# An attention and maxout kernel: a branch on the head flags, with two key blocks per query block for the odd heads in one arm

## The chip, the cores and the metric

The kernel runs on one core of a Trainium2 chip. The metric is the device time of that core in microseconds, from the first to the last instruction of one execution. Five engines work side by side: TensorE (PE in the profile; its weight loads are listed apart as PEld), VectorE (DVE), ScalarE (ACT), GpSimd (POOL) and SyncE (SP), which here only issues transfers. Each engine takes its instructions in the order in which they are written. Transfers are issued by SP, ACT and POOL and carried by 16 DMA engines.

## The reference

Causal attention for 4 batches, 8 heads, 768 positions and a head size of 64 is followed by a maxout layer. A head that is flagged as a retrieval head sees all earlier positions. Any other head, a streaming head, sees the first 4 positions (the sink) and the last 64 (the window).

```python
is_retrieval = np.array([1, 0, 1, 0, 0, 0, 1, 0])
n_sink, window = (4, 64)
causal = rel >= 0                       # rel = query position - key position
stream_keep = causal & (is_sink | ((rel >= 0) & (rel < window)))
scores = np.where(mask, scale * q @ k.T, -1e9)     # mask: causal, or stream_keep, by head
a = exp(scores - max) / (sum + 1e-9)
x = (a @ v) as 3072 tokens x 512
out = maximum(maximum(x @ w1, x @ w2), x @ w3) @ w_out      # 512 -> 768 -> 512
```

The flags are an input of the kernel, so what is computed must hold for any flags. In these inputs heads 0, 2 and 6 are retrieval heads, and all odd heads and head 4 are streaming heads.

## The kernel before

**Tiles.** A batch is cut into two halves of 384 queries, and a half into three query blocks of 128. Keys lie in blocks of 128 too. Work on the scores is numbered by t = 4 * batch + 2 * half + qd, where qd names one of two groups of four heads; a group holds two pairs of heads, i = 0 and 1. Scores are made with keys in the rows and queries in the columns. A score unit (`scores`, L553 for the matmuls) computes up to 512 such columns for each head of the group; which key and query blocks stand in which unit is told by `UNITS`. One half's causal triangle has 6 blocks in two units, the second half's has 15 in four. In batch 0 two heads of a pair use 64 rows each of the array side by side; in the other batches four heads use 32 rows each, and a block takes two passes (head size 64 = 2 x 32), which add up in PSUM. ScalarE then takes the exponential of a unit and writes fp16 (`pt`, L564).

**Masks.** `mk` holds a mask of 512 columns for each head, made from the head's flag (L389). VectorE or GpSimd multiplies the blocks near the diagonal and at the start with it (`masks`, L586). For the far blocks of streaming heads the values are scaled instead: `vf` is the values times `far`, which is zero there but for the sink's rows (`prep_v`, L504 and L506). So one instruction stream serves all flags, and streaming heads compute all of their causal blocks.

**Values and layer.** `av` (L602) multiplies a weight tile, a 128x128 block of `pt`, with 65 columns of values (the last is a one, for the sum), over all key blocks up to the query block, and divides (L610, L612). The result is turned by a DMA transpose (L621) or by TensorE (`turn_x`), and feeds the layer: `ffn` (L438 for the three projections, L455 and L458 for the maximum, L474 for the output product, L480 for the copy to the output tile).

**Order.** Nothing is scheduled at build time: `PROGRAM` is an order written out item by item, and each item issues its instructions on its engines at that place. `s t u i` is a score unit, `k` a mask, `v` the preparation of values, `av` the product with the values, `x` the turning, `f` the next piece of the layer, which fills TensorE between score units, `load`, `load_v` and `hl` are loads, `w` weights, `turn` and `turnp` the turning of keys and queries, `em` and `m` the masks for each head, `idle n` runs n matmuls on zeros. Loads of batch 0 and of all values go through SP's queue; weights, and the keys and queries of the other batches, through GpSimd's. Tiles come from pools that are used in turn.

Of the kernel before, what the change touches and what calls it, by code (L numbers as in the profile page):

```python
# [37 lines left out]

APART = [(0, 0, 1, (384,), 128, 0), (1, 1, 1, (384,), 128, 0)] + MASKED[1][1:]


EARLY = 0

FIRST = "hl 0 0 1, ir"

PROGRAM = (
    "idle 2, idle 8, cast 0 0 aa, hl 0 1 1 ss, hl 0 2 2 ss, read, hl 1 0 2 ss, cast 0 1 pp",
    "flags, cast 0 2 ap, em 1, turnp 0 1 a, far, em 0, turnp 0 0 aa, cast 0 3 da, em 2, em 3",
    "load_v 0 0 4 4, s 0 0 1, s 0 0 0, v 1 1 pp, cast 1 1 pa, turnp 0 3 dd, turnp 0 2 da",
    "w 0 2 0, load_v 0 0 0 4, v 0 0 dp, s 1 0 0, w 0 2 1, s 0 1 0 b, hl 1 2 2 ss, s 1 0 1",  # L50
    "cast 1 2 dp, v 1 0 dd, s 0 1 1, s 1 1 0 b, av 0 0, v 0 1 pp, turnp 1 1 a, s 1 1 1",
    "turnp 1 2 aa, x 0 0 a, s 2 0 1, cast 1 0 dp, load_v 0 1, cast 1 3 ad, av 1 1, s 2 1 1",
    "av 1 0, x 1 1 d, av 0 1, turnp 1 0 ad, s 2 2 1, x 1 0 d, s 3 0 0, m 0, w 1, x 0 1 d",
    "s 2 0 0, m 3, m 1, f 1 d, f 1 d, s 2 1 0, s 2 2 0, m 2, f 1 a, f 1 d, k 2 1 2 p, k 2 0 1 d",
    "w 2, f 1 d, s 2 3 1, load 1 0, w 3, k 3 0 0 d, s 3 1 0, f 1 a, s 2 3 0, load 1 1",
    "k 2 0 3 p, k 2 0 2 p, turnp 1 3 dd, k 3 0 1 p, k 2 1 1 d, k 2 1 3 d, f 1 d, f 1 d",
    "v 2 0 ad, f 1 a, f 1 a, v 3 1 pp, f 1 d, s 3 0 1, v 2 1 dp, s 3 1 1, f 1 a, v 3 0 ap",
    "av 2 0 D, f 1 d, f 1 d, s 3 2 0, turn 1 0 0 0, turn 1 0 0 1, f 1 a, turn 1 0 1 0, s 3 2 1",
    "s 3 3 0, k 3 0 2 p, k 3 1 2 p, turn 1 0 1 1, f 1 a, av 2 1 D, s 3 3 1, k 3 1 1 d",
    "k 3 0 3 p, k 3 1 3 p, f 1 a, k 3 1 0 d, load_v 1 0, gate, f 1 a, s 4 0, k 4 1 0 p",  # L60
    "v 4 0 pp, av 3 0, av 3 1, f 1 a, f 1 a, x 3 0 d, s 4 1, turn 1 1 0 1, x 3 1 a, f 1 d",
    "v 5 1 pp, turn 1 1 1 0, turn 1 1 1 1, turn 1 1 0 0, k 4 0 1 d, k 4 0 0 d, k 4 1 1 p, f 1 a",
    "f 1 a, f 1 d, load_v 1 1, f 1 a, f 1 a, f 1 a, v 4 1 pd, f 1 a, f 1 d, s 5 0, f 1 a, f 1 d",
    "av 4 0 D, k 5 0 0 d, f 1 d, s 5 1, k 5 0 1 p, load_v 2 0, f 1 a, f 1 a, load 2 0, f 1 a",
    "s 6 0, f 1 d, av 4 1 D, f 1 a, v 5 0 ap, f 1 a, s 6 1, f 1 a, av 5 0 D, f 1 d, f 1 d",
    "k 5 1 1 p, k 5 1 0 p, v 7 0 dp, s 6 2, k 6 1 2 p, f 1 a, av 5 1 D, turn 2 0 1 0, f 1 a",
    "v 6 0 ad, s 6 3, turn 2 0 0 1, x 5 1 d, f 1 a, turn 2 0 1 1, load 2 1, load 3 1",
    "load_v 2 1, v 6 1 ap, f 1 d, f 1 d, k 6 0 2 p, v 9 0 ap, k 6 1 3 p, f 1 a, f 1 a",
    "turn 2 0 0 0, s 7 0, f 1 a, f 1 d, f 1 d, turn 2 1 0 0, k 6 0 1 d, f 1 a, s 7 1, f 1 d",
    "f 1 a, f 1 a, k 6 1 1 p, k 7 1 1 d, f 1 d, s 7 2, f 1 a, f 1 a, k 6 0 3 p, k 7 1 2 d",  # L70
    "turn 2 1 1 0, load 3 0, av 6 0 D, s 7 3, f 1 d, v 7 1 pp, av 6 1 D, k 7 1 3 p, f 1 d",
    "turn 3 1 1 0, k 7 0 3 p, turn 2 1 0 1, s 8 0, k 7 0 1 p, turn 2 1 1 1, k 7 0 2 p, f 1 a",
    "f 1 d, load_v 3 0, k 8 0 0 p, av 7 1 D, s 8 1, f 1 a, f 1 a, s 9 0, v 8 0 ap, k 8 0 1 d",
    "f 1 a, f 1 d, av 7 0 D, v 13 1 pp, s 9 1, f 1 a, av 8 0 D, f 1 d, s 10 0, f 1 a, x 7 1 d",
    "f 1 a, v 10 0 dd, f 1 d, s 10 1, f 1 a, f 1 d, v 9 1 ad, f 1 a, f 1 d, f 1 a, s 10 2",
    "f 1 d, f 1 d, f 1 d, k 8 1 0 p, f 1 d, k 9 0 0 p, k 9 1 1 d, f 1 d, f 1 d, v 11 0 ad",
    "f 1 d, k 9 1 0 p, v 12 0 ad, k 9 0 1 p, k 8 1 1 d, av 9 0 D, v 8 1 ap, s 10 3, f 1 d",
    "f 1 a, av 8 1 D, turn 3 0 1 0, s 11 0, k 10 1 1 p, f 1 d, f 1 d, k 10 0 3 p, f 1 a",
    "av 9 1 D, v 13 0 ap, f 1 a, k 10 1 3 d, turn 3 0 1 1, x 9 1 a, k 10 0 1 p, s 11 1, f 1 a",
    "k 10 0 2 p, v 11 1 ap, av 10 0 D, f 1 d, s 11 2, k 11 0 2 p, turn 3 0 0 0, f 1 a",  # L80
    "turn 3 0 0 1, f 1 d, k 11 0 1 d, f 1 a, k 10 1 2 d, f 1 d, v 10 1 ap, f 1 a, turn 3 1 0 1",
    "f 1 a, f 1 a, s 12 0, av 10 1 D, f 1 a, f 1 d, k 12 1 0 p, s 12 1, f 1 d, f 1 a, f 1 a",
    "k 12 0 1 p, turn 3 1 0 0, s 11 3, v 12 1 ad, f 1 a, load_v 3 1, f 1 a, f 1 a, k 11 0 3 d",
    "k 11 1 3 p, f 1 d, f 1 d, k 11 1 1 p, turn 3 1 1 1, f 1 a, f 1 d, av 11 0 D, f 1 d",
    "k 11 1 2 d, f 1 a, k 12 0 0 p, k 12 1 1 d, f 1 a, s 13 0, av 12 0 D, f 1 d, av 11 1 D",
    "k 13 0 0 d, f 1 d, f 1 d, s 13 1, f 1 d, v 15 1 pp, f 1 d, k 13 0 1 p, x 11 1 d, f 1 d",
    "v 15 0 ad, av 12 1 D, k 13 1 1 d, av 13 0 D, s 15 0, f 1 a, f 1 d, f 1 d, f 1 a, f 1 d",
    "f 1 d, f 1 a, k 13 1 0 d, s 15 1, v 14 0 ap, f 1 d, f 1 a, f 1 d, f 1 d, s 14 0, f 1 a",
    "f 1 d, f 1 d, f 1 d, av 13 1 D, s 14 1, f 1 d, x 13 1 d, f 1 d, f 1 d, f 1 a, f 1 a",
    "s 14 2, f 1 a, k 14 1 2 p, v 14 1 ad, k 14 1 1 p, f 1 d, f 1 d, f 1 d, f 1 a, f 1 a",  # L90
    "k 15 0 1 p, s 14 3, f 1 d, k 14 0 3 p, f 1 a, f 1 d, s 15 2, f 1 a, f 1 d, f 1 d, f 1 d",
    "s 15 3, f 1 a, k 15 1 1 d, f 1 a, k 15 1 3 d, f 1 a, k 15 1 2 d, k 14 0 1 p, f 1 a",
    "k 14 0 2 p, k 14 1 3 p, k 15 0 3 d, av 14 0 D, f 1 a, f 1 a, f 1 a, av 14 1 D, f 1 a",
    "f 1 d, k 15 0 2 p, av 15 1 D, f 1 a, av 15 0 D, f 1 d, x 15 1 d, f 1 a, f 1 d, f 1 a",
    "f 1 d, f 1 d, f 1 a, f 1 a, f 1 a, f 1 d, f 1 a, f 1 a, f 1 d, f 1 d, f 1 a, f 1 d, f 1 a",
    "f 1 a, f 1 a, f 1 a, f 1 a, f 1 d, f 1 a, f 1 d, f 1 a, f 1 d, f 1 a, f 1 d, f 1 a, f 1 a",
)

# [11 lines left out]
def kernel(  # L110
# [14 lines left out]
    nc = tc.nc  # L125
# [14 lines left out]
    assert (S, D, DMdl) == (768, 64, 512) and window <= P and n_sink <= P  # L140
# [5 lines left out]

    consts = ctx.enter_context(tc.tile_pool(name="consts", bufs=1))
    stage = ctx.enter_context(tc.tile_pool(name="stage", bufs=3))
    pairs2 = ctx.enter_context(tc.tile_pool(name="pairs2", bufs=2))
    once = ctx.enter_context(tc.tile_pool(name="once", bufs=1))  # L150
    half16 = ctx.enter_context(tc.tile_pool(name="half16", bufs=3))
    qkt = ctx.enter_context(tc.tile_pool(name="qkt", bufs=3))
    ptp = ctx.enter_context(tc.tile_pool(name="ptp", bufs=5))
    xp = ctx.enter_context(tc.tile_pool(name="xp", bufs=4))
    xtp = ctx.enter_context(tc.tile_pool(name="xtp", bufs=3))
    htp = ctx.enter_context(tc.tile_pool(name="htp", bufs=2))
    accp = ctx.enter_context(tc.tile_pool(name="accp", bufs=7))
    fwork = ctx.enter_context(tc.tile_pool(name="fwork", bufs=3))
    sps = ctx.enter_context(tc.tile_pool(name="sps", bufs=2, space=bass.MemoryType.PSUM))
    bkp = ctx.enter_context(tc.tile_pool(name="bkp", bufs=4, space=bass.MemoryType.PSUM))  # L160

    ctx.enter_context(tc.manual_schedule())


# [5 lines left out]
    def bank(shape, dtype, name):  # L170
        return bkp.tile(shape, dtype, tag="bank", name=name)

    staged = {}
    cast = {}
    KQs = {}

    def load_pairs(half, hp, n, engines):
        for nm, src, eng in zip(("ks", "qs"), (k, q), engines):  # L180
            st = (
                pairs2.tile([P, 4, HB, D], FP32, tag=nm, name=nm) if n == 2
                else once.tile([P, 2 * n, HB, D], FP32, name=f"{nm}{hp}")
            )
            m = 2 * n if eng is nc.gpsimd else 2
            for h in range(0, 2 * n, m):
                eng.dma_start(  # L187
                    out=st[:, h : h + m],
                    in_=src[
                        0, 2 * hp + h : 2 * hp + h + m, half * HALF : (half + 1) * HALF  # L190
                    ].rearrange("h (p j) d -> p h j d", p=P),
                )
            for i in range(n):
                staged.setdefault((half, hp + i), []).append(st[:, 2 * i : 2 * i + 2])

    def load_cast(half, hp, n):
        for nm, src in (("kc", k), ("qc", q)):
            st = half16.tile([P, 4, HB, D], FP16, tag=nm, name=nm)
            nc.gpsimd.dma_start(
                out=st[:, 0 : 2 * n],  # L200
                in_=src[
# [215 lines left out]
    def ffn(b, half):  # L417
# [31 lines left out]
        if early:  # L449
            yield  # L450
# [265 lines left out]
```

## Time and profile before

| | |
|---|---|
| Median of 3 runs | 200.72 us (199.87 to 202.32) |
| The profiled execution | 199.87 us; span 199.9 us, so nothing lies around the span |
| Mean granted clock of TensorE | 0.990 of full speed |
| Bytes | 25.17 MB read from HBM, 6.29 MB written |
| Value products (L602) | 352 with `va` and 320 with `vf` |
| Score matmuls (L553) | 560 |
| Masks of `pt` (L586) | 54 on GpSimd, 57.3 us; 32 on VectorE, 14.3 us |
| Exponentials (L564) | 98, 83.3 us |

In the profile's lists a group of instructions has its busy time, in which instructions that overlap on a pipelined engine count once, and the mean duration of one, which for matmuls holds the whole way through the array. The chain that ended last is shown in pieces: start, length, engine, tile and line. On an engine that is always busy the lengths of these pieces are what a group really costs in time.

### The profile page before, as it was taken

To read this page: it belongs to the slowest core of one execution; us is meant where nothing else is said; L and a number is where in the kernel's file an instruction comes from. 1 tells how busy PE (TensorE), PEld (TensorE's weight loads), DVE (VectorE), ACT (ScalarE), POOL (GpSimd) and SP (SyncE) were. 2 spreads that over 40 slices of the span, in tenths; PEclk is the share of its full clock that TensorE was granted. 3 is DMA by queue.
4 is the path that set the end of the run, shared out by engine and by line. 5 is a ranking of instruction groups with operands and counts; after the bars stand their busy time and mean duration, and the time that the engine had idled before them with its cause. 6 is when DMAs were issued, how large, how long until landed. Compare 5 with 4: busy or idle time off the path is not lost.

```text
span 199.9 us, 5135 instructions
## 1 busy us (share of the span) xinstructions
PE 190.0 (95%) x2059; PEld 109.3 (55%) x2059; DVE 148.3 (74%) x311; ACT 115.9 (58%) x171; POOL 90.5 (45%) x118
## 2 busy tenths in 40 slices
PE   7688898999999999999999999999999999999993
PEld 2345444565556455666456645574656455765552
DVE  3638965998976789896469998996978288767750
ACT  4489983765658798687776756634366565100011
POOL 3429187583276598490697245652010197000000
PEclk9889999999999999999999999999999999999999
DMA  5999999995979989988521232703500120124004
GB/s 143 312 245 230 196 195 212 208 169 76 283 173 211 162 169 208 218 218 176 147 76 23 43 124 74 159 20 73 167 5 20 53 108 0 23 59 157 3 0 157
DMA packets 48429, 26.48 MB, mean 132 GB/s; under 512 B 36758, under 2 KB 43926, under 8 KB 48406
## 3 DMA queue, kind: packets, MB, share of 16 engines
q1 hardware_dynamic: 43366, 17.96, 37.9%
q0 software_dynamic: 4624, 7.87, 21.9%
q8 instruction: 16, 0.26, 0.6%
q10 hardware_dynamic: 416, 0.33, 0.5%
q14 instruction: 7, 0.06, 0.1%
HBM read 25.17 MB, written 6.29 MB: 157 GB/s over the span
## 4 chain that ended last, share of the span: by engine, by line
PE 75%; DMA 11%; DVE 4%; SPq 3%; issue 2%; ACT 2%; POOL 0%; DVEq 0%
PE yy L438 39%; PE yy L474 14%; PE st L553 9%; PE oacc L602 9%; DMA vs<-in_v_dram 7%; PE yst L438 3%; DMA qs<-in_q_dram 2%; DVE KQ L267 2%; SPq L187 2%; ACT pt L564 1%; DMA xT<-x 1%; PE yst L474 1%; DVE acc L458 1%; DVE hT L458 1%; SPq L621 1%
## 5 line engine op out<-in xcount | busy, mean ns | idle before, releaser
L564 ACT ACTIVATE pt<-st 128x1024 f16<-128x1024 f32 (+3 forms) x98 | 83.3, 905 | 33.0 <-PE st L553 31.0
L586 POOL TENSOR_TENSOR pt<-pt,mk 128x512 f16<-128x512 f16 (+1 forms) x54 | 57.3, 1088 | 38.4 <-ACT pt L564 20.1
L438 PE MATMUL yy<-xT,w1t 128*128 128x384 f16 x180 | 35.8, 327 | 1.2 <-DVE pt L586 1.2
L438 PE MATMUL yy<-xT,w2t 128*128 128x384 f16 x180 | 36.1, 326 | 0.0
L438 PE MATMUL yy<-xT,w0t 128*128 128x384 f16 x180 | 35.8, 327 | 0.3
L458 DVE TENSOR_TENSOR acc<-yy,acc 128x384 f16<-128x384 f32 x45 | 24.8, 557 | 10.7 <-PE yy L438 8.6
L474 PE MATMUL yy<-woutt,hT 128*128 128x512 f16 (+1 forms) x138 | 31.6, 375 | 0.0
L553 PE MATMUL st<-KQ 32*128 32x384 f16 (+5 forms) x560 | 29.4, 281 | 1.4 <-ACT pt L564 0.8
L458 DVE TENSOR_TENSOR hT<-yy,acc 128x384 f16<-128x384 f32 x45 | 24.8, 556 | 4.5 <-PE yy L438 2.3
L602 PEld LDWEIGHTS <-pt 128*128 128x128 f16 x672 | 24.4, 97 | 4.8 <-DVE va L504 0.7
L267 DVE STREAM_TRANSPOSE KQ<-kq 128x384 f32<-128x384 f32 x24 | 25.5, 1132 | 0.6 <-DMA kq<-in_q_dram 0.6
L602 PE MATMUL oacc<-va,pt 128*128 128x65 f16 x352 | 24.9, 193 | 0.5 <-DVE va L504 0.5
L438 PEld LDWEIGHTS <-w1t 128*128 128x128 f16 x192 | 17.5, 98 | 14.1 <-issue 1.6
L438 PEld LDWEIGHTS <-w0t 128*128 128x128 f16 x192 | 17.8, 98 | 13.4 <-issue 0.8
L438 PEld LDWEIGHTS <-w2t 128*128 128x128 f16 x192 | 17.3, 98 | 11.9 <-issue 1.4
L553 PEld LDWEIGHTS <-KQ 32*128 32x128 f16 (+1 forms) x560 | 12.2, 93 | 18.8 <-issue 11.8
L474 PEld LDWEIGHTS <-hT 128*128 128x128 f16 x150 | 13.8, 98 | 14.7 <-issue 0.8
L602 PE MATMUL oacc<-vf,pt 128*128 128x65 f16 x320 | 21.1, 193 | 0.0
L455 ACT CAST acc<-yy 128x384 f16<-128x384 f32 x25 | 12.0, 481 | 13.9 <-PE yy L438 13.5
L612 DVE TENSOR_TENSOR x<-oacc,rc 128x384 f16<-128x384 f32 x32 | 17.8, 557 | 1.1
L480 DVE COPY ot<-yy 128x512 f32<-128x512 f32 (+1 forms) x15 | 10.1, 675 | 9.2 <-PE yy L474 9.2
L506 POOL TENSOR_TENSOR vf<-va,far 128x384 f16<-128x384 f16 x10 | 8.6, 867 | 17.3 <-ACT va L504 12.9
(72 smaller groups left out, 143.4 us busy)
## 6 DMA issues: line engine op xcount, KB each, us to landing
out_dram<-ot SPq DMA_DIRECT2D x23, 256.0 KB, 2.1
vs<-in_v_dram SPq DMA_DIRECT2D x21, 256.0 KB, 5.6
kq<-in_k_dram POOLq DMA_DIRECT2D x6, 384.0 KB, 7.9
kq<-in_q_dram POOLq DMA_DIRECT2D x6, 384.0 KB, 10.0
ks<-in_k_dram SPq DMA_DIRECT2D x8, 192.0 KB, 3.6
qs<-in_q_dram SPq DMA_DIRECT2D x7, 192.0 KB, 4.8
vs<-in_v_dram SPq DMA_DIRECT2D x6, 128.0 KB, 4.8
w0t<-in_moe_w_dram POOLq DMA_DIRECT2D x2, 384.0 KB, 9.4
```

What stands on the lines that cost most here:

```text
L267: nc.vector.transpose(out=dst.rearrange("c (p j) -> c j p", j=n)[:, j0:j1], in_=src.rearrange("c (j i) -> c j i", i=R),)
L438: nc.tensor.matmul(yy[:, 0:HALF], w_t[wi][:, ks, ni * P : (ni + 1) * P], xT[b, half][ks].rearrange("p a t -> p (a t)"), start=(ks == 0), s ...
L455: copy_out[0](out=acc[ni], in_=yy[:, 0:HALF])
L458: nc.vector.tensor_tensor(out=dst, in0=yy[:, 0:HALF], in1=acc[ni], op=ALU.max)
L474: nc.tensor.matmul(yo[:, 0:n], hT[ns][:, tb * P : (tb + 1) * P], woutt[:, ns, c : c + n], start=(ns == 0), stop=(ns == NNB - 1),)
L480: op(out=ot[:, c : c + n], in_=yo[:, 0:n])
L506: vf_engine.tensor_tensor(out=vf[j][:, hs, k0:k1, 0:D], in0=vs[:, hs, 0:1] if half == 0 else va[j][:, hs, k0:k1, 0:D], in1=far[:, hs, k0:k ...
L553: nc.tensor.matmul(sts[g // m][:, g % m, c0 : c0 + n * P], KQ[rows, 0, ki * P : (ki + 1) * P], KQ[rows, 1, t0 : t0 + n * P], start=(c0 == ...
L564: nc.scalar.activation(out=pts[t, i][:, u, h0 : h0 + m, 0:w], in_=st[:, :, 0:w], func=AF.Exp, scale=sc,)
L586: engine.tensor_tensor(out=x, in0=x, in1=m, op=ALU.mult)
L602: nc.tensor.matmul(o[:, qi, hl, 0 : D + 1], pt[:, u, hl, c : c + P], vv[:, 2 * hp + hl, ki, 0 : D + 1], start=(idx == 0), stop=(idx == len ...
L612: nc.vector.tensor_tensor(out=x, in0=o[:, :, :, 0:D], in1=rc.unsqueeze(3).to_broadcast([P, HB, 2, D]), op=ALU.mult,)
```

## The change

The diff below is cut to its core. It does the following.

- A first part of the order (`FIRST`) is the same for all flags. In it VectorE compares the flags with the set 1,0,1,0,0,0,1,0 (`compare_flags`), all five engines read the result into a register (`number`), and then each branches: to `NEAR` if the flags are this set, to `ANY` if they are not. Both arms hold all the rest of the work. `NEAR` lies right behind the branch; at its end the engines jump over `ANY`.
- Heads are regrouped: group qd = 0 holds the even heads and qd = 1 the odd ones (`pair`), head h with head h + 4. Weight rows are loaded in two halves of 64 partitions to fit this.
- In `NEAR`, from t = 2 on, an odd head's query block takes two key blocks: its own, and a joined block whose first 64 rows are the first 64 keys and whose other 64 rows are the last 64 keys of the block before (`join_k`, `join_v` build these from keys and values). In batches 1 to 3 the three units of the first half's t cover both halves of the batch. One mask `NM` serves them all.
- Also in `NEAR`, head 4 leaves out the value products of the blocks between the first and the last two, heads 0, 2 and 6 use plain values, and the pair 2, 6 is masked with the plain triangle (`WHOLE`).
- Tiles get fixed buffers (`Turns`), given back by hand, so that both arms begin from the same state; the layer's state is kept in a dictionary for the same reason.
- `FIRST`, `NEAR` and `ANY` are new orders.

```diff
+FIRST = (
+    "cast 0 0 0 a, hl 0 1 1 1 s, read, cast 0 1 1 a, hl 0 2 2 0 s, hl 0 2 2 1 s, hl 1 2 2 1 s",
+    "idle 8, cast 0 2 1 a, load_v 0 0 0, flags, cast 0 2 0 d, em 0, em 3, differ, cast 0 0 1 p",
+    "turnp 0 0 aa, number, turnp 0 2 ad, far, idle 2, v 0 0 p",
 )
+
+NEAR = (
+    "em 2, cast 0 3 1 a, cast 0 3 0 a, s 0 0 0, hl 0 1 1 0 s, vf 0 0 p, cast 0 1 0 p",
+    "turnp 0 3 ad, idle 3, em 1, cast 1 2 1 d, w 0 2 0, hl 1 2 2 0 s, cast 1 2 0 d, s 1 0 0",
...
+    def pair(qd, i):
+        return slice(2 * i + qd, 2 * i + qd + G + 1, G)
+
+    def nearly(t):
+        return near[0] and t >= NQ
...
+    def compare_flags():
+        nc.vector.tensor_tensor(out=other, in0=RT1, in1=known, op=ALU.not_equal)
+        nc.vector.tensor_reduce(
+            out=others, in_=other, op=ALU.max, axis=mybir.AxisListType.X
+        )
...
+            for m in range(2):
+                nc.gpsimd.dma_start(
+                    out=w_t[wi][m * D : m * D + D, :, c : c + n],
...
+    def join_k(b, rows, i, op):
...
+        blocks = of_pair(NQ + i)[:, 0].rearrange("p (a t) -> p a t", t=D)
+        op(
+            out=pair_joins(i)[:, :, to],
+            in_=blocks[:, 5:10:2] if rows else blocks[:, 0:1].to_broadcast([P, HB, D]),
+        )
+
+    def join_v(b, part, rows, op):
+        j, n = b % 2, D
+        k0, k1 = ((0, 1), (1, 4))[part]
+        r = slice(rows * n, rows * n + n)
+        op(
+            out=vf[j][r, 1::2, k0:k1, 0:D],
+            in_=va[j][r, 1::2, k0 + 1 : k1 + 1, 0:D] if rows
+            else va[j][r, 1::2, 0:1, 0:D].to_broadcast([n, G, k1 - k0, D]),
+        )
+
...
+    def group(t, u):
...
+        b, half, qd = where(t)
+        if not (nearly(t) and qd == 1):
+            return [(*part, 0) for part in UNITS[half][u]]
+
+        if half == 0:
+            todo = [(0, 0)] + [(qi, joined) for qi in range(1, NSB) for joined in (1, 0)]
+        else:
+            todo = [(qi, joined) for qi in range(HB, NSB) for joined in (0, 1)]
...
     def masks(t, i, u, engine):
         b, half, qd = where(t)
         pt = pts[t, i]
+        if nearly(t) and qd == 1:
...
             engine.tensor_tensor(out=x, in0=x, in1=m, op=ALU.mult)
+            return
...
+    def products(t, i):
...
+                if nearly(t) and qd == 1:
+                    pt = pts[t - (NQ if b > 0 and half == 1 else 0), i]
+                    own, joined = (2 * q, 2 * q - 1) if b > 0 else (2 * qi, 2 * qi + 1)
+                    if q > 0:
+                        yield qi, m, pt, divmod(joined * P, 512), (
+                            va[j][:, h, 0] if q == 1 else vf[j][:, h, q - 2]
+                        )
+                    yield qi, m, pt, divmod(own * P, 512), va[j][:, h, q]
+                    continue
+                for ki in range(q + 1):
+                    if nearly(t) and h == G and 0 < ki < q - 1:
+                        continue
...
+    do["number"] = lambda: number.append(nc.values_load(others, min_val=0, max_val=1))
+    run(FIRST)
+    states = [dict(x) for x in kept_state]
+    queued = [dict(z, acc=dict(z["acc"]), hT=dict(z["hT"])) for z in queue]
+    with tc.If(number[0] < 1, preferred_fallthrough_block=True) as known_set:
+        near[0] = True
+        run(NEAR)
+        while queue:
+            fill(1)
...
+    with known_set.Else():
+        near[0] = False
+        run(ANY)
```

## The prediction

> **What bounds the kernel.** I read the shares of the engines first, then the slices of the span, then the stretches, then the chain in order of time. Engines and slices:
>
> ```profile
> PE 190.0 (95%) x2059; PEld 109.3 (55%) x2059; DVE 148.3 (74%) x311; ACT 115.9 (58%) x171; POOL 90.5 (45%) x118
> ...
> PE   7688898999999999999999999999999999999993
> ...
> DMA  5999999995979989988521232703500120124004
> ```
>
> TensorE (PE) is the busiest engine, and its only weak slices (5 us each) are the first eight and the last. The transfers are dense until about 95 us and thin later. Three stretches (busy us of PE, PEld, DVE, ACT, POOL with counts, clock, DMA share, GB/s) separate the two regimes:
>
> ```profile
> 30.00:35.00 5.00, 4.03 (x29) 2.25 (x30) 2.83 (x7) 1.68 (x4) 3.88 (x5) 1.00 1.13 212
> ...
> 70.00:80.00 10.00, 10.00 (x105) 5.42 (x104) 8.70 (x13) 8.72 (x14) 9.24 (x13) 1.00 0.99 189
> ...
> 140.00:150.00 10.00, 10.00 (x117) 5.87 (x114) 8.65 (x20) 5.17 (x6) 0.83 (x1) 1.00 0.27 83
> ```
>
> From 35 to 197 us TensorE is full at the whole clock, so a piece of its work taken out there shortens the span unless a new wait enters. The first 35 us go at the pace of the transfers. Start, length and work of pieces of the chain:
>
> ```profile
> 15.53 14.68 DMA vs<-in_v_dram
> ...
> 68.21 0.45 PE st L553 x8
> 68.67 2.70 PE yy L474 x12
> 71.36 0.56 PE st L553 x16
> ...
> 77.91 0.57 PE st L553 x16
> 78.47 1.41 PE yy L438 x8
> 79.88 0.94 PE oacc L602 x30
> ...
> 86.52 0.34 PE st L553 x8
> 86.86 1.41 PE yy L438 x8
> ...
> 182.39 0.65 PE yst L438 x4
> ```
>
> This is the price list. Thirty attention-times-value matmuls (oacc) take 0.94 us, 31 ns each; the group's mean of 193 ns contains the pipeline. A score unit (st) costs its piece and 0.11 us more in the projection (yy) behind it: eight of those take 1.41, where two fours of 0.65 make 1.30. Its length follows its blocks of 128x128 scores: with two blocks (x8 of 256 columns) 0.34, three 0.45, four (x16) 0.57. One block goes through in two steps of four heads side by side, so a step is 0.055 us, and a unit is 0.23 us fixed (0.12 in the piece, 0.11 behind it) plus its steps.
>
> **What leaves TensorE** (counted in the two built programs, by the known-set arm, which the flags 1,0,1,0,0,0,1,0 take).
> - Values: 672 to 492 matmuls, 180 x 31 ns = **5.6 us**.
> - Scores of batches 1 to 3, odd heads: before, 21 blocks in 6 units, 42 x 0.055 + 6 x 0.23 = 3.7 us a batch; after, 11 blocks in 3 units, 22 x 0.055 + 3 x 0.23 = 1.9. Three batches: **5.4 us**.
> - Scores of batch 0, second half, odd heads: two pairs of 15 blocks in 8 units become two of 6 in 4. A step there is one block of one pair (two heads side by side): 18 x 0.055 + 4 x 0.23 = **1.9 us**.
>
> Sum 12.9 us. The unsafe part is the step. Now almost every step needs fresh weights (128 columns instead of up to 384 behind one load). No row shows a long run of 128-column steps. Nearest above is the value matmul, which loads 128x128 for each 65 columns: 31 ns a pair of instructions, so at worst a step of four pairs is 0.124 us, and one of batch 0, with two pairs, 0.062. Then a batch takes 22 x 0.124 + 0.69 = 3.4 instead of 1.9, batch 0 still saves 1.8, and the sum is 5.6 + 0.8 + 1.8 = 8.2. The low end is 0.055, as the x16 unit already holds two 128-column steps behind each other at that price; I take it. The Trainium skill ("TensorE: Matmul & The Clock Gate", section LDWEIGHTS) gives a load as columns / 1.2 GHz whatever the rows, an estimate of 107 ns for 128 columns. By that a batch's scores would be 22 x 0.107 + 0.69 = 3.0 us and save 0.7; the 31 ns of the value pairs, each with such a load, speak against it here.
>
> **What is added or moved.**
> - Masks of the joined units are wider (1024 columns on DVE, estimated 1.0 us from 522 ns for 512, ten of them; four on POOL at an estimated 2.3 from 1.17), but fewer; sixteen exponentials of 1.03 us go from ACT, far-key scalings of 0.44 to 0.87 us from POOL and of 0.35 to 0.74 from DVE; joins of keys and values come (about 20 copies, 0.4 to 1.0 by the casts of 384 at 0.5). By these rows DVE falls by some 9 us, ACT by 17, POOL by 8. They lie beside TensorE; the 70 to 80 us stretch, POOL 9.24 of 10, is where one could surface. Cost 0, up to 2.
> - Seven more idle matmuls, 0.2 to 0.4 us each: in the first 35 us TensorE waits anyway, cost 0; without that cover 1.5 to 2.8.
> - Weights come in eight issues instead of four, 0.8 us of POOL each: +3.3 us on its queue between 15 and 40 us, beside scalings that leave. 0 to 2, taken 0.
> - **The branch.** Each engine waits for a word that DVE makes, reads it into a register and branches; everything behind it in order waits, SP's loads too. In this trace the flags reach DVE at 4.10 and the per-head limits end at 5.81. Behind them now stand a key cast (0.54), four mask rows (4 x 0.385), a compare and a reduction (0.2 each): 8.3 at the earliest, 10.0 if the key transfer lands at 7.5 as here; I take 9. No row shows the register read: 0.1 (a tiny DVE operation) to 2.8 (the flags' transfer, issue to use); taken 0.5, near the first, as it passes no DMA queue. So SP stands from about 7.5 (eleven issues of 0.5 and some held) to 9.5. Here SP issued six value loads in 7.54 to 11.99. Its transfers outstanding, up to eight of 192 KB at 311 GB/s = 5 us, cover the stop only in part, and first exponentials come at about 11 instead of 9.85. I charge 1.5 once (0 to 3).
> - The end: engines jump over the other arm before the last waits. The jump lies beside the last output's 2.0 us landing; 0.3 (0 to 2).
> - Seams: TensorE finishes 5 to 6 us earlier at 95 us while DMA engines are near 1.0 there. The trace shows 0.6 us of one wait for a batch's keys, so slack exists: taken 1.0 (0 to 4). A new order may also close gaps (-2).
>
> **Sum**: 199.9 - 12.9 + 1.5 + 0.3 + 1.0 = 189.8, against the profiled span 199.9, which is the execution's own time (199.87), nothing lying around it. The median of the three runs is 0.8 higher, so I forecast **190.5** as median; the case spans 187 to 193.5.
>
> **Rivals.**
> - *Small steps bound the scores* (31 ns a pair): 8.2 instead of 12.9 saved, 194.5, as median **195.3**. For it: twice the instructions per column. Against: groups of four start together in the x16 units. Chance 0.10.
> - *Transfers bound the first half*: with DMA at 0.97 to 1.16 of the engines until 90 us, TensorE cannot run ahead, and only what is saved after about 95 us counts, half of 12.9: 199.9 - 6.5 + 1.8 = 195.2, **196**. For it: the slices of DMA. Against: no wait of TensorE for a transfer after 36 us but 1.4 + 0.7 us for weights early on, and the thin last half shows that loads run ahead. Chance 0.12.
> - *Slower: the arm's instructions are fetched late.* If the branch throws away what was fetched ahead, five engines fetch blocks behind full DMA queues, where loads here take 4.8 us (values, on SP) to 18.5 us (output weights, on POOL) to land. Everything stands meanwhile. Over 11 us of it eats the gain; at 18.5 the time is 189.8 + 17, about **207**. For it: DMA is full just then. Against: the known arm stands right behind the branch, and the trace's 23 packets of instructions caused no visible stop. The Trainium skill ("Runtime: NRT & Kernel Launch", section Instruction fetch mechanics) says a taken branch out of the two-block window stalls for a DMA fetch, a falling-through one is not named; only the jump at the end is taken here. Chance 0.08.
> - *The known arm isn't taken*: the other arm does the former work behind a branch, 199.9 + 1.8, **202.5**. The flags equal the known set, so 0.02.
> - *Better*: new order fills the startup as well, below **187**: 0.08.
>
> The forecast has 0.60. **Range 187 to 197.5**: forecast, both partial cases, some 0.82. Two per cent, about what these runs tell from no change, is 196.7 and 204.7 around the median 200.72. Faster: forecast, better, and over half of the two partial cases, 0.82. Slower: most of the fetch case, 0.06. Same: 0.12.
>
> **What would show it.** After: PE matmuls about 1,890 and the share still above 90%; oacc pieces at 31 ns; a joined x32 unit at 0.57 (0.124 a step: above 1.0); ACT near 99 us, DVE near 139; first exponential near 11 us; TensorE full from about 36 us to 3 us before the end. A wait on a transfer after 40 us would show the second rival, engines silent right after the branch the third. I am wrong if the startup is over 5 us longer, or if gaps open between 40 and 95 us.

## The result, and the profile after

The changed kernel takes **221.11 us** (median of 4, 220.05 to 224.63); the kernel before, on the same chip, 200.83. The ratio is 1.098, with a 95% interval of 1.0915 to 1.1046: **ten per cent slower**, where 190.5 us and "faster" were forecast, and outside the range of 187 to 197.5. (Medians and ranges here are of all executions, ratios of the undisturbed ones.) The profiled execution took 220.46 us with a span of 218.6. Some 1.7 to 1.9 us lie around the span in every execution of both kernels for which both are on record, so the earlier reading of the kernel before, a span of 199.9 beside a time of 199.87, is not borne out.

The page of the changed kernel, shares and slices of 5.5 us (PEclk is the granted clock in tenths):

```profile
PE 188.7 (86%) x1906; PEld 107.1 (49%) x1906; DVE 141.6 (65%) x288; ACT 100.1 (46%) x156; POOL 80.1 (37%) x112
...
PE   7399993199699996996999939999999999999990
...
PEclk9999999569969999699999985999999999999999
```

The work fell as forecast: 1,906 matmuls (about 1,890 expected), ScalarE 100.1 us (99), VectorE 141.6 (139). But TensorE has holes until past the middle of the span, and behind most of them the granted clock falls. Stretches (busy us of PE, PEld, DVE, ACT, POOL with counts, clock, DMA share, GB/s):

```profile
35.00:40.00 5.00, 0.00 (x0) 0.00 (x0) 0.43 (x1) 0.00 (x0) 0.00 (x0) 0.73 1.27 144
40.00:50.00 10.00, 7.23 (x55) 3.85 (x55) 4.62 (x8) 3.63 (x6) 5.27 (x8) 0.62 0.54 71
```

From 35 to 40 us nothing computes but one operation of VectorE, though the DMA engines are counted as busy. After 140 us TensorE is full, as forecast. What TensorE waited for (us in total, times, longest):

```profile
PE bank L851 <- ACT va L639: 7.9, 1, 7.9
PE bank L578 <- DMA xT<-x: 4.8, 4, 2.4
...
PE bank L340 <- DVE others L520: 3.4, 1, 3.4
```

The first is a cast that stands for the transfer of batch 0's last values (a last 4-byte packet of SyncE's queue ends at 41.4 us, the cast starts at 42.2), the last is the branch. Transfers are 26% of the chain (start, length, what):

```profile
16.86 14.28 DMA vs<-in_v_dram
...
80.85 6.94 DMA xT<-x
```

A transpose (xT) of 6.9 us stands out: its median from issue to landing is 2.4. The clue lies in the lists of queues and issues. First of the kernel before, then of the changed one (packets, MB, share; for issues KB and median us from issue to landing):

```profile
q0 software_dynamic: 4624, 7.87, 21.9%
...
kq<-in_k_dram POOLq DMA_DIRECT2D x6, 384.0 KB, 7.9
kq<-in_q_dram POOLq DMA_DIRECT2D x6, 384.0 KB, 10.0
```

```profile
q0 software_dynamic: 9296, 7.88, 25.0%
...
kq<-in_k_dram POOLq DMA_DIRECT2D x6, 384.0 KB, 14.5
kq<-in_q_dram POOLq DMA_DIRECT2D x6, 384.0 KB, 14.5
```

The same bytes come in twice the packets, and the median load lands 1.5 to 1.8 times as late. The regrouping of heads changed `load`, the transfer of keys and queries of batches 1 to 3. Four heads that lie behind one another in memory were one run of 128 rows; every second head is four blocks of 32 rows:

```diff
-                in_=src[b, G * qd : G * qd + G].rearrange("h (p j) d -> (h p) j d", p=R),
+                in_=src[b, qd::NQ].rearrange("h (p j) d -> h p j d", p=R),
```

Counted from the packets of 3,072 bytes in the trace, such a load of the changed kernel occupies 4.0 DMA engines (47.5 to 48.5 us), and 8.6 where keys and queries overlap; before, it was 15 to 16 at the height of a load. The extra packets have 4 bytes: some 400 for each load instead of 16. The Trainium skill ("DMA: Bandwidth & Descriptors", section "Why a DMA increments its semaphore by 16 and not by 1") states that the number of engines is the largest, up to 16, that divides the size of the slowest dimension on both sides; that is 4 for four heads against 128 partitions and 16 for 128 rows. The trace agrees, with 4.0 and with 15 to 16. Whether the few engines or the extra small packets cost more is not separated by any run here, as each edit below changes both; the 4-byte packets of this queue take 77 us, summed over all engines, against 4 before.

### The profile page after: what moved, and what is told of

Same layout as the page of the kernel before. It is cut to its first block, busy times and chain, and to the rows that moved or that the text cites. A ratio compares the mean times of both kernels' runs of the same rounds, so it can differ in the third digit from the quotient of the medians.

```text
span 218.6 us, 4813 instructions
## 1 busy us (share of the span) xinstructions
PE 188.7 (86%) x1906; PEld 107.1 (49%) x1906; DVE 141.6 (65%) x288; ACT 100.1 (46%) x156; POOL 80.1 (37%) x112
## 4 chain that ended last, share of the span: by engine, by line
PE 46%; DMA 26%; DVE 9%; issue 7%; SPq 6%; POOL 3%; ACT 1%; POOLq 0%; DVEq 0%
PE bank L578 25%; DMA vs<-in_v_dram 18%; PE bank L611 9%; DMA xT<-x 6%; SPq L396 4%; PE bank L851 4%; PE st L763 4%; PE st L578 3%; DVE hT L591 2%; DMA ks<-in_k_dram 2%; DVE KQ L375 2%; DVE pt L795 1%; POOL pt L813 1%; DVE acc L591 1%; POOL pt L795 1%
## 5 line engine op out<-in xcount | busy, mean ns | idle before, releaser
L774 ACT ACTIVATE pt<-st 128x1024 f16<-128x1024 f32 (+2 forms) x72 | 63.0, 922 | 39.2 <-PE st L763 39.0
L578 PE MATMUL bank<-xT,w0t 128*128 128x384 f16 x180 | 37.5, 338 | 4.8 <-DMA xT<-x 4.8
L578 PE MATMUL bank<-xT,w1t 128*128 128x384 f16 x180 | 35.9, 330 | 2.6 <-DVE hT L591 2.1
L578 PE MATMUL bank<-xT,w2t 128*128 128x384 f16 x180 | 37.8, 339 | 0.3 <-DVE x L865 0.3
L591 DVE TENSOR_TENSOR acc<-bank,acc 128x384 f16<-128x384 f32 x45 | 24.9, 555 | 20.3 <-PE bank L578 11.6
L611 PE MATMUL bank<-woutt,hT 128*128 128x512 f16 (+1 forms) x138 | 33.8, 394 | 0.0
L851 PE MATMUL bank<-va,pt 128*128 128x65 f16 x409 | 21.0, 196 | 11.7 <-ACT va L639 7.9
L591 DVE TENSOR_TENSOR hT<-bank,acc 128x384 f16<-128x384 f32 x45 | 24.8, 558 | 4.4 <-PE bank L578 1.5
L763 PE MATMUL st<-KQ 32*128 32x128 f16 (+4 forms) x468 | 21.9, 267 | 0.0
L813 POOL TENSOR_TENSOR pt<-pt,mk 128x512 f16<-128x512 f16 (+1 forms) x12 | 13.8, 1152 | 7.8 <-ACT pt L774 7.8
L763 PEld LDWEIGHTS <-KQ 32*128 32x128 f16 (+1 forms) x472 | 10.1, 96 | 12.2 <-issue 9.3
```

The costliest lines, as they stand in the source:

```text
L578: nc.tensor.matmul(yy[:, 0:HALF], w_t[wi][:, ks, ni * P : (ni + 1) * P], xT[b, half, ks].rearrange("p a t -> p (a t)"), start=(ks == 0), s ...
L591: nc.vector.tensor_tensor(out=dst, in0=yy[:, 0:HALF], in1=acc[ni], op=ALU.max)
L611: nc.tensor.matmul(yo[:, 0:n], hT[ns][:, tb * P : (tb + 1) * P], woutt[:, ns, c : c + n], start=(ns == 0), stop=(ns == NNB - 1),)
L763: nc.tensor.matmul(sts[x][:, c0 : c0 + n * P], keys, KQ[rows, 1, t0 : t0 + n * P], start=(c0 == 0 and r == 0 and not early), stop=(b == 0 ...
L774: nc.scalar.activation(out=pts[t, i][:, u, m0:m1, 0:w], in_=sts[i, m0][:, 0:w].unsqueeze(1) if apart else sts[i][:, :, 0:w], func=AF.Exp, ...
L813: engine.tensor_tensor(out=x, in0=x, in1=m, op=ALU.mult)
```

## The experiments

Two theories stood at first: the spread over four engines (S), and a bad order of GpSimd's early issues (O).

**1. Four transfers for each load.** The changed kernel, each load cut into one transfer per head, 32 rows each.

```diff
-            nc.gpsimd.dma_start(
-                out=st[:, i],
-                in_=src[b, qd::NQ].rearrange("h (p j) d -> h p j d", p=R),
-            )
+            for g in range(G):
+                nc.gpsimd.dma_start(
+                    out=st[R * g : R * g + R, i],
+                    in_=src[b, qd + NQ * g].rearrange("(p j) d -> p j d", p=R),
+                )
```

> Edit: in the changed kernel each load of keys or queries of batches 1 to 3 (one transfer over four heads that lie apart) is written as four transfers, one for each head, of 32 rows each. The bytes, the tile and the place in the order stay. Theory S (spread): in the changed kernel such a load keeps only 4 of the 16 DMA engines busy (4.0 engines at 48 us, 8.6 when keys and queries run together, where the kernel before shows 15.5), so it lands in 14.5 us instead of 7.9 to 10.0 and other queues' transfers wait behind it on those engines. S expects 188 to 197 us here, 14 to 16 engines at work on these loads, and no wait of TensorE of over 3 us after 45 us. Theory O (order): the new order lets transfers collide whatever their form. O expects 215 to 222 us.

Measured: 202.23 us (12 executions, 199.87 to 206.73), ratio to before 1.0027 (0.9984 to 1.0071). Nineteen of the twenty lost us come back, loads land in 5 to 6 us with some 16 of their packets under way at a time, and TensorE's longest wait after 45 us is 2.7 us. So the signs of S are there, but the time stops 5 us above its range.

**2. The strided form alone, in the kernel before.** Only the line of `load` shown above is changed; it loads the even and the odd heads where heads 0 to 3 and 4 to 7 belong.

> Edit: in the kernel before, the loads of keys and queries of batches 1 to 3 take every second head (one transfer over four heads that lie apart), as in the changed kernel; nothing else. The heads of batches 1 to 3 are then exchanged against their values and flags, so the output is another one, but every instruction has the same size. Theory S expects that this alone makes the kernel before slower by 8 to 25 us (208 to 225), with these loads at 4 to 9 engines and landing after 13 us or more. Theory O expects 199 to 203.

Measured: 233.37 us (229.42 to 236.16) against 200.46, **33 us more** by the medians and 29 by the lowest execution, beyond what S expected. Stretches of this run, and the piece of its chain that covers them:

```profile
80.00:90.00 10.00, 0.98 (x14) 0.28 (x7) 7.84 (x6) 2.84 (x4) 5.75 (x7) 0.70 1.26 100
90.00:100.00 10.00, 0.48 (x1) 0.10 (x1) 0.00 (x0) 0.00 (x0) 2.52 (x4) 0.50 1.14 114
```

```profile
79.39 21.94 DMA xT<-x
```

For twenty us TensorE does next to nothing: it waits three times, 19.9 us together, for transposes on SyncE's queue, while strided loads run on GpSimd's. So the form slows not only its own loads (here 21 to 23 us to land) but also what other queues send at that time. O is refuted as the main cause.

**3. Without the branch.** Kernel 1 with the known arm straight on: no register read, no branch, no second arm, so it serves this set of flags alone.

> Edit: the kernel with four transfers a load, and the branch left out: no register read, no second arm, the known-set arm follows the first part of the order at once, so it is right for these flags alone; the comparison of the flags stays. If the branch costs what its wait shows in the changed kernel (first exponential at 12.03 instead of 9.85 us, SyncE idle from 7.6 to 9.6), this is 1 to 3 us faster than the kernel with four transfers. If the branch is free beside the transfers, within 0.7 us of it.

Measured: 199.81 us (196.8 to 201.7), ratio to before 0.9867 (0.9764 to 0.9969); by the medians 2.4 less than kernel 1.

**4. Four transfers in the kernel before.** The edit of kernel 1, with the heads as they were. Now the theories were P (GpSimd's queue) and T (TensorE's work mis-sized).

> The kernel before, in which each load of keys or queries of batches 1 to 3 goes out as four transfers of one head each: 48 issues on GpSimd instead of 12, nothing else changed. Theory P (what is left of the loss in the changed kernel with four transfers per load, 202 against the forecast 190.5, comes from GpSimd's queue: 36 more issues at 0.5 us are 18 us on an engine that is at 9.24 of 10 at 70 to 80 us, and its masks stand behind them): 202 to 206. Theory T (TensorE's work was forecast too small, or gaps of the new order have nothing to do with these issues): 199.5 to 201.5.

Measured: 221.31 us, ratio 1.1017 (1.0932 to 1.1102): **20 us more, far above even P**. GpSimd's own timeline in this run (start, length, operation, count; in brackets what it stood waiting for):

```profile
26.66 2.01 POOL L252 DMA_DIRECT2D kq<-in_k_dram  x4
28.63 1.01 POOL L252 DMA_DIRECT2D kq<-in_q_dram  x2
31.15 0.49 POOL L252 DMA_DIRECT2D kq<-in_q_dram  x1 [1.51 <-DMA w1t<-in_moe_w_dram]
...
43.98 0.49 POOL L252 DMA_DIRECT2D kq<-in_q_dram  x1 [4.15 <-DMA woutt<-in_moe_w_out_dram]
44.49 2.89 POOL L587 TENSOR_TENSOR pt<-pt,mk 128x512 f16<-128x512 f16 x3
```

Two weights, four loads of keys and two of queries are out: eight. The ninth issue stands until the oldest weight has landed, and the next one 3.4 us more for the other weight; at 44 us, behind the output weights, the same. (Whether the chip or the program's own semaphores set the eight is not shown here.) Behind the standing issue wait masks, and TensorE waits 16.1 us in three times for masks ("oacc", for `pt` on GpSimd). So the price of an issue is not its 0.5 us but the place of the oldest of eight transfers.

**5 and 6. GpSimd's order in kernel 1.** First the early part (third weight later and in two halves, loads of batch 1 behind the masks), then also the later loads one place earlier.

```diff
-    "... turnp 1 0 ad, w 2, cast 1 1 0 p, ..."
+    "... k 3 0 0 p, w 2 2 0, ... k 2 0 1 p, w 2 2 1, ... v 3 1 p, w 3, ... c 0 1 0 p, load 1 0"
-    "... f 1 a, load 1 1, k 2 1 0 p ..."
+    "... k 3 1 1 p, load 1 1, av 3 1 ..."
# and, in the second of the two, too:
+    "... load 2 0, v 4 1 p ...", "... c 1 0 0 p, load 2 1, v 8 0 p ...", "... v 9 1 d, load 3 0, s 6 3 ..."
```

> The changed kernel with four transfers per load (202.2 us), with the early part of the known arm's order changed on GpSimd's queue alone: the third weight goes out some 6 us later and in two halves, behind the first masks; the first two loads of keys and queries and the output weights go out behind the masks and casts that value products wait for. Theory P with contention (values of batch 0 land at 39 us beside weights, and masks stand behind loads: TensorE idle 3.6 of 5 us at 35 to 40 and 2.2 at 40 to 50): 197 to 200. Theory T: 201 to 203, no change.

> As the kernel with the early part changed, and the loads for batches 2 and 3 go out one place earlier each: the first where GpSimd is idle at 50 to 60 us, the others one place on. Theory P (the 8.9 us transfer of queries at 81 and the 2.7 us of TensorE's idle time at 90 to 93, with the clock of 0.66 behind it, come from loads that are issued late): 2 to 4 us less than with the early part alone, 194 to 197. Theory T: the same time as with the early part alone.

Measured: 207.64 (204.05 to 208.95) and 207.52 us (207.07 to 210.63), above both answers and slower than kernel 1; moving the later loads too changed nothing. TensorE is full from 30 to 38 us as P wanted, the values have landed by 31.6 instead of 39.0, and then it waits 4.8 us for batch 1's keys, which now come late. The gap was moved, not closed: P named a real wait but not a free place for the loads.

**7. Contiguous loads in the changed kernel.** The cleanest test of the form: the changed kernel with the line of `load` from before. In batches 1 to 3 it computes with the wrong heads, at the same sizes, so it serves for the time alone.

> The changed kernel, in which the loads of keys and queries of batches 1 to 3 take four heads that lie behind one another in memory, as the kernel before does: one transfer, one issue, the same bytes. It loads heads 0 to 3 and 4 to 7 where the even and the odd heads belong, so in batches 1 to 3 it computes with the wrong heads; every instruction and every byte is otherwise that of the changed kernel. Theory S (the form of these loads, and with four transfers their issues, is the whole of what the prediction missed): 188 to 194. Theory B (the other terms fell short as well: transfers bound the first 50 us, or GpSimd's order): 195 to 199. If neither, above 200.

Measured: median 203.08 us, but four executions of 196.22, 202.56, 203.6 and 204.07: by the median neither theory (the lowest lies in B's range), and no interval can be given. The profiled one (203.6) again has a wait of 9.3 us for values at 35 us.

**8. The same without the branch.**

> As the changed kernel with contiguous loads (wrong heads in batches 1 to 3), and without the branch, the register read and the second arm. The branch's price, 2.4 us beside four transfers per load, should come out again: 1.5 to 3 us less than with the branch, whatever the time of that is; S 186 to 192, B 192 to 197.

Measured: **191.23 us** (190.37, 190.94, 191.52, and one of 201.42), ratio to before 0.9509 (0.9402 to 0.9616). The time lies in S's range, and the branch's price is not 2.4 us here but 5 (against the lowest execution with it) to 12 (against the median). Its page, then a piece of its chain:

```profile
PE 180.4 (95%) x1906; PEld 104.4 (55%) x1906; DVE 142.4 (75%) x288; ACT 99.9 (53%) x156; POOL 78.0 (41%) x112
...
PE   7699999998999999997999999999999999999993
```

```profile
92.45 0.57 PE st L763 x32
```

TensorE is full, its longest wait for a transfer is 1.4 us, the joined unit of 32 matmuls takes the 0.57 us of the forecast, thirty value products 0.95. Why does a branch of 2 us cost up to 12? SyncE's last value issues of batch 0, with the branch (the traced execution of experiment 7) and without (start, length over three issues), and the cast on ScalarE that these values release:

```profile
14.60 8.17 SPq L396 DMA_DIRECT2D vs<-in_v_dram  x3
...
42.97 0.51 ACT L639 CAST va<-vs 128x384 f16<-128x384 f32 x1 [11.95 <-issue]
```

```profile
13.42 4.33 SPq L396 DMA_DIRECT2D vs<-in_v_dram  x3
...
31.90 0.51 ACT L639 CAST va<-vs 128x384 f16<-128x384 f32 x1 [1.82 <-issue]
```

Without the branch the third issue is out at 17.75 us, before the third weight (20.3). With it, it is out at 22.77, behind that weight (21.4). From there values, in packets of 256 bytes, share the engines with packets of 1,536: from 28 to 31 us 110 to 121 value packets leave in a us beside 103 to 112 weight packets, so values get about a seventh of the bytes. The cast comes 11 us later.

**9. A middle order in kernel 1**: only half of the third weight and the output weights later, loads of batch 1's first group in place, those of its second group behind two masks.

```diff
-    "... turnp 1 0 ad, w 2, ...", "... k 3 1 0 d, w 3, k 2 0 2 d, ..."
+    "... turnp 1 0 ad, w 2 2 0, ...", "... k 2 0 1 p, w 2 2 1, ... c 0 1 0 p, w 3, ..."
# and "load 1 1" moves behind "k 3 1 1 p"
```

> The changed kernel with four transfers per load and a middle order of GpSimd's early issues: the loads of batch 1's first group stay where they were (moving them behind the masks made TensorE wait 4.8 us for keys); only the second half of the third weight and the output weights go behind the masks, and the second group's loads behind the two masks at 46 us. If GpSimd's queue (masks behind loads, loads behind eight outstanding transfers) is what holds TensorE at 35 to 50 us: 197 to 200. If the transfers themselves bound that stretch, a shifted gap, and 201 to 204.

Measured: 203.73 us (202.09 to 204.74), ratio 1.0149. Values have landed by 34, and TensorE waits 3.8 us for the output weights instead: the gap was shifted, as the second answer expected.

**10 to 12. Is the branch's price the late values?** Theory V says yes; R says that the stop or the fetching of code costs it. With contiguous loads: four of SyncE's loads issued ahead of the branch; or the third weight issued later. And the latter with four transfers and the right heads.

```diff
-    "turnp 0 0 aa, number, turnp 0 2 ad, far, idle 2, v 0 0 p",
+    "turnp 0 0 aa, hl 0 1 1 0 s, load_v 0 0 1, number, turnp 0 2 ad, far, idle 2, v 0 0 p",
# and "hl 0 1 1 0 s" and "load_v 0 0 1" go from the two arms
```

```diff
-    "... turnp 1 0 ad, w 2, cast 1 1 0 p, ..." , "... k 3 0 0 p, s 2 1 0, ..."
+    "... turnp 1 0 ad, cast 1 1 0 p, ..." , "... k 3 0 0 p, w 2, s 2 1 0, ..."
```

> As the changed kernel with contiguous loads (wrong heads in batches 1 to 3; 196.2 to 204.1 us, median 203.1), with four of the loads that stood behind the branch on SyncE, one of keys and three of values, issued ahead of it. Theory V (the branch costs 5 to 12 us here, not 2, because SyncE stands until 9.6 us and its later value loads of batch 0 fall behind the weights: they land at 43 us instead of 32, and TensorE waits 9.3 us for them): 191 to 195, with the last values of batch 0 by 34 us. Theory R (the stop of the engines itself, or code that is fetched late, costs the time): 199 to 204.

> As the changed kernel with contiguous loads (wrong heads in batches 1 to 3), with the third weight issued some 6 us later on GpSimd, so that it does not come ahead of batch 0's last value loads. Theory V: values land by 34 us and the time is 192 to 196; the wait of 9.3 us is gone, unless the weight itself is now late (a wait of TensorE for w2t at 38 to 45 would show it). Theory R: 199 to 204.

> The changed kernel with four transfers per load (202.2 us, the right heads), with the third weight issued some 6 us later on GpSimd and nothing else moved. Theory V: the values land by 34 us, the wait for them goes, and the time is 196 to 200, as far as GpSimd's 48 issues leave it. Theory R: 201 to 204.

Measured: 195.40 (194.54 to 197.87), ratio 0.9728 (0.9662 to 0.9795), and 196.31 us (195.64 to 197.46), ratio 0.9788 (0.9713 to 0.9864). In both the values land early (cast at 32.6 and 30.8 us), the wait for them is gone, and no execution is above 198. R falls as the whole of the price; V fits, 0.4 and 0.3 us above its ranges. It is shown for the execution of experiment 7 that was traced (203.6): the lowest, 196.22, has no trace, and it is as fast as these two without any repair, and what spared it stays open. So do the 4 to 5 us that are left against experiment 8. The third gives 202.53 us (200.15 to 206.09), ratio 1.0044, the time that R named: the values have landed by 31.3 us there too, but TensorE then waits for masks and joined values on GpSimd (2.8 and 2.2 us), which stand behind the issues of the loads, as in experiment 4.

**13 and 14. All repairs together**: loads ahead of the branch, the weight later, and eight masks, casts and joins of 30 to 50 us moved from GpSimd to VectorE or ScalarE. With four transfers per load, and with the changed kernel's strided load.

```diff
-    "... k 2 0 1 p, s 2 0 1, v 3 0 p ...", "... k 2 1 1 p, s 2 1 1, c 0 1 1 p, c 0 1 0 p ..."
+    "... k 2 0 1 d, s 2 0 1, v 3 0 a ...", "... k 2 1 1 d, s 2 1 1, c 0 1 1 d, c 0 1 0 d ..."
```

> The changed kernel with four transfers per load and the right heads (202.2 us), with three repairs of the known arm's early order: four of SyncE's loads ahead of the branch, the third weight some 6 us later, and nine masks, casts and joins between 30 and 50 us taken from GpSimd, where they stand behind the loads' issues, to VectorE or ScalarE. If what is left of the loss is what stands behind those issues (TensorE waited 2.8 us for a mask and 2.2 us for joined values on GpSimd between 33 and 45 us with the weight moved alone): 195 to 199, faster than both kernels at the low end. If the 48 issues and their transfers bound that stretch in another way (keys late, the eight transfers outstanding): 200 to 204.

> The changed kernel as it is, with its one strided transfer per load, and the same three repairs of the order. If the strided transfers themselves (4 of 16 engines, and other queues' transfers held behind them) are the larger part of the loss, the repairs gain only the wait for batch 0's values and little more: 210 to 218. If order and branch were the larger part: below 206.

Measured: 203.36 us median of 13 (199.19 to 205.39), ratio 0.9969 (0.9905 to 1.0032), so the second answer; GpSimd's last load of queries stands again:

```profile
POOL kq L358 <- DMA woutt<-in_moe_w_out_dram: 5.0, 1, 5.0
```

And with the strided load **226.47 us** (225.13 to 231.34), ratio 1.1244, slower than unrepaired and above both answers. What VectorE waited for in that run:

```profile
DVE KQ L375 <- DMA kq<-in_k_dram: 17.0, 3, 11.4
```

This repair of the order does not help the strided form, which is the larger part of the loss by itself. A version with the right heads that is clearly faster than the kernel before, for any flags, was not found. The only one ahead of it, kernel 3, serves one set, by 1.3% with an interval that almost reaches 1.

## Why the prediction was wrong

The 30.6 us between 190.5 and 221.1 come apart by the medians of the runs (the executions of experiment 7 spread over 8 us; with its lowest, 196.2, the last two terms would be +3.2 and +24.9, so the form is the largest either way): without branch and with contiguous loads 191.2 where 190.5 - 1.8 = 188.7 was forecast, **+2.5**; the branch 203.1 - 191.2 = 11.9 instead of 1.8, **+10.1**; the form of the loads 221.1 - 203.1 = **+18.0**, instead of nothing. What makes up the 2.5 was not taken apart.

- **What leaves TensorE: right.** In experiment 8 TensorE is busy 9.6 us less than before (190.0 to 180.4), although the idle matmuls grow from 4.0 to 7.3 us; the rest of its work falls by 11.6 us by the trace (12.9 if no idle matmul overlaps another), where 12.9 was counted. The seven more idle matmuls, costed at nothing, come to 0.5 us each instead of 0.2 to 0.4; how much of that the time pays was not measured. The time falls by 8.6 us against the runs beside it. The step of 0.055 us and the 31 ns held. The rival of small steps (31 ns a pair, a unit above 1.0 us) is refuted by the 0.57 us. The estimate of 107 ns a step, worked out from the Trainium skill ("TensorE: Matmul & The Clock Gate", section LDWEIGHTS), is refuted by the same row: eight steps of it would be 0.86.
- **Masks and joins at 0: right**, with contiguous loads. Weights in eight issues "0 to 2, taken 0": no wait for them shows in experiment 8.
- **Seams, "taken 1.0 (0 to 4)", is the step that failed most.** It weighed the bytes that flow and the slack of one wait for keys. But the change moved no bytes; it changed how a load lies in memory. The weights' new issues were costed, the line of the keys' and queries' load never, and it makes +18.0 here. That line, changed alone in the kernel before, costs 29 to 33 us there; its loads run on 4 engines instead of 16 in the changed kernel.
- **The branch, "I charge 1.5 once (0 to 3)", was mis-sized** (5 to 12 us). Its parts were right: the register read took 0.5 us (flags at 8.59, TensorE on at 9.13), SyncE stood from 7.57 to 9.57, the first exponential came at 12.0 (11 forecast). What was missing is what the delay does to order: value loads that were ahead of a weight fall behind it. The transfers outstanding, 5 us of them, were said to "cover the stop only in part"; in the traced execution they cover nothing for what is issued behind it, which loses its place.
- **The rival "transfers bound the first half" (196, chance 0.12)** was the right kind: waits for transfers after 40 us showed, as it said. Its mechanism was not: with contiguous loads and no branch, TensorE is full from 10 us on beside the same dense transfers.
- **The slower rival, late instruction fetch,** is refuted at the size it was given: TensorE goes on 0.54 us behind the word, and with the loads moved ahead the branch costs 195.4 - 191.2 = 4 us in all, of which TensorE's own wait is 2.8.

## What to carry to other kernels

A diff that renumbers heads, rows or tiles is also a change of every access pattern that takes them. Price each transfer by how its slowest dimension splits over the engines, and by its number of issues, before its bytes. Splitting a bad transfer into good ones is no free repair where the issuing engine has other work: in these kernels, with eight outstanding, the next issue, and all behind it, waits for the oldest. And a stop in front of loads should be priced by what they may fall behind, and not by its length alone.

## What was not expected of the hardware

- Beside loads on few engines other queues' packets take long. In the changed kernel one 4-byte packet of SyncE's queue took 6.4 us (35.0 to 41.4), and eight output packets of 2,048 bytes 3.6 to 3.9 us each at 56; in experiments 1, 7, 8 and 10 to 13 not one packet took over 3 us.
- Idle time costs twice. The same 1,906 matmuls are 188.7 busy us at a mean granted clock of 0.944 and 180.4 at 1.00 in experiment 8: 8.3 of the 20 us that the change lost are work at a lower clock, in and behind the holes. The clock is 0.50 in stretches around 38 to 47, 61.5 to 64.5, 89 to 91.5 and 130 to 136 us, where the projections' matmuls take 512 ns on average, against 327 in the rest.
